# A three-layer kernel on one core: another order for its prologue, and two VectorE operations of the first blocks on GpSimd

## The chip, the cores and the metric

The kernel runs on one core of a Trainium2 chip. The metric is the device time of one execution in microseconds, as the median of several runs. A core has five engines with a queue each: TensorE (matrix products into PSUM), VectorE and ScalarE (element by element, on SBUF and PSUM), GpSimd (element by element, on SBUF), and SyncE, whose queue issues the transfers between HBM and SBUF. A queue issues in order. Engines wait for one another through semaphores, which the framework sets.

## The reference

Three layers in float32: chunked attention over 4 x 8 heads of 768 positions, then a layer with a squared ReLU, then a gated one.

```python
for c in range(nc):                       # chunks of 32; q, k, v: (4, 8, 768, 64)
    ...
    k_full = concatenate([mem_k, k_ctx], axis=2)      # 8 memory keys + up to 56 of the context
    scores = scale * matmul(q_c, k_full.T)
    a = exp(scores - max(scores))
    a = a / (sum(a) + 1e-9)
    out[:, :, c_start:c_end] = matmul(a, v_full)
x = out.transpose(0, 2, 1, 3).reshape(3072, 512)
h = maximum(x @ w_in, 0); y = (h * h) @ w_out         # 512 -> 2048 -> 512
g = y @ w_gate; z = (g * sigmoid(g) * (y @ w_val)) @ w_out2   # 512 -> 1536 -> 512
```

## The kernel before

Each large product is made of three products of float32r numbers: an operand is split into a high half (a cast, on ScalarE) and a low half (the difference, a subtraction), and high x high, high x low and low x high are summed in PSUM. In the names `whi`/`wlo` are the halves of a weight, `xh`/`xl` those of x, `gh`/`gl` those of the square. `split` (line 74) makes both halves: the cast is line 76, the subtraction line 79, whoever calls it.

**Attention.** The 32 groups of 96 queries are units; four units make a block of 384 tokens, and there are eight blocks. A unit u has these steps, each a function: `at_load` (queries and keys, 464 KB, one tile `qk`), `at_load_v` (values, 256 KB, two tiles), `at_scores` (48 small products, line 136; then VectorE's fills of masked columns), `at_max` (VectorE: maximum and its scaling, lines 148 and 149), `at_exp` (ScalarE: eight exponentials with their sums, line 157), `at_norm` (VectorE: two small instructions for the inverse sums, lines 171 and 172, and the multiplication of the probabilities by them, line 173), `at_turn` (VectorE: seven transposes of 32x32 blocks into `pT`, line 178), `at_pv` (16 products, line 197, into `abank`), `at_split_x` (ScalarE copies x out of `abank`, VectorE forms its low half). Probabilities have two tiles in turn; `abank` has one place for the weighted sum. Scores of the first block's units lie in two other PSUM tiles in turn, those of later units in `abank`.

**The first feed-forward layer.** For each block t and each of 16 slices f of 128 hidden columns, `hidden(t, f)` makes 12 products (line 264), then ScalarE applies ReLU (line 271), squares it twice (272, a float32r value, and 273), and VectorE subtracts for `gl` (line 274). `project(t, f)` makes 12 products (line 295), of which the last third uses `gl`. `hidden` runs two slices ahead of `project`. A slice's weight comes as 64-bit numbers: `load_w` fetches 1 MB into one of two tiles `raw` (line 84), `convert` turns it to float32 by an activation on ScalarE (line 94), a shift (line 95) and a combination (line 97) on VectorE, called a cut here, into one of two tiles `cut`; `split` then makes the 2 x 1024 columns of `whi` and `wlo`. `load1(f)` and `prep1(f)` do this for slice f; all 16 pairs of weights stay in SBUF through the eight blocks, in the 32 tiles of the pool `wp`. `spare()` takes a tile of this pool for something else.

**What sets the order.** Python code emits the instructions, and the framework's scheduler orders them by priority (the earlier emitted first) and by its own estimate of when an instruction is ready. Inside a region `manual_schedule` the engines that it names issue in the order of emission; where other instructions fall between these stays the scheduler's. Before, such a region held TensorE from block 1 on and all engines in the gated layer. The prologue (lines 541 to 562) emits, unit by unit, the four units of block 0, the loads of the first weights and `prep1(0)`. After it, before the first `hidden`, come the plans' steps below zero: `plan` holds the attention of the units 4 to 31, `wplan` the weights. Four steps make a round of one `hidden` and one `project`; a unit's steps stand at fixed lags (`LAGS`) about its step `e` (line 232): loading 24 before, scores 16 before, maximum 14 before, weighted sum at 0. For the units 4 to 7 (block 1), whose attention runs in block 0, e is 1, 17, 33 and 49. `prep1(f)` stands at step 4(f - 4), four rounds ahead of its use, for f of 1 to 3 at the start.

The gated layer (lines 427 and on) has GpSimd form the low halves of its weights (`split_w`, 128x512 and 128x384).

Of the kernel before, what the change touches and what calls it, by code (L numbers as in the profile page):

```python
# [7 lines left out]
F32 = mybir.dt.float32  # L8
# [3 lines left out]
ALU = mybir.AluOpType  # L12
# [6 lines left out]
GQ = 96  # L19
# [3 lines left out]
NH = 8  # L23
# [24 lines left out]
def attention_moe_moe_kernel(ctx, tc, att, w1, w2, out):  # L48
# [25 lines left out]
    def split(hi, lo, src, hi_engine, lo_engine):  # L74
        if hi_engine is act:
            act.copy(hi, src)  # L76
        else:
            hi_engine.tensor_copy(hi, src)
        lo_engine.tensor_tensor(lo, src, hi.bitcast(F32), ALU.subtract)  # L79
# [31 lines left out]

    def at_load(u):
        t, g = units[u]
        raw = st[u]["raw"] = ap.tile([128, UQ + UK], F32, tag="qk", name="qk")
        sp.dma_start(out=raw, in_=att[g, :, 0:UQ + UK])

    def at_load_v(u):
# [50 lines left out]
    def at_norm(u):  # L168
        sm = st[u].pop("sm")
        p = probs[u % 2][:, :, 0:WK]  # L170
        dve.tensor_scalar(sm, sm, 1e-9, None, ALU.add)
        dve.reciprocal(sm, sm)
        dve.tensor_tensor(p, p, sm.to_broadcast([GQ, NH, WK]), ALU.mult)  # L173

    def at_turn(u, chunks=range(3)):
        for c in chunks:
# [52 lines left out]
    nunit = BLOCKS[0]  # L229
    for t, n in enumerate(BLOCKS[1:], 1):  # L230
        for j in range(n):
            e = QB * (t - 1) + (j + 1) * QB // n - 15
            for lag, fn in LAGS:
                plan.setdefault(e + lag, []).append((lag, fn, nunit))
            nunit += 1
# [10 lines left out]
    def pair(pool_, tag):  # L246
        return [pool_.tile([128, 1024], R, tag=tag, name=n) for n in ("whi", "wlo")]

    def load1(f):
        w["raw", f] = load_w(w1[f])  # L250

    def prep1(f):
        w[f] = pair(wp, "w")
        split(*w[f], convert(w.pop(("raw", f))), act, dve)

    def hidden(t, f, between):
        n = nt_of[t]
        whi, wlo = w[f]
        xh, xl = xt[t]
        hps = hbank[next(turn) % 2][:, 0:n]  # L260
        i = 0
        for wt, x in ((whi, xh), (whi, xl), (wlo, xh)):
            for k in range(KD):
                pe.matmul(hps, wt[:, k * 128:(k + 1) * 128], x[:, k, 0:n], start=i == 0, stop=i == 3 * KD - 1)  # L264
                i += 1
                if i == 6:
                    between()
        r = gp.tile([128, NTM], F32, tag="r", name="r", bufs=2)[:, 0:n]
        gh = gp.tile([128, NTM], R, tag="gh", name="gh", bufs=3)[:, 0:n]
        gl = gp.tile([128, NTM], R, tag="gl", name="gl", bufs=3)[:, 0:n]  # L270
        act.activation(r, hps, AF.Relu)  # L271
        act.activation(gh, r, AF.Square)
        act.activation(r, r, AF.Square)  # L273
        dve.tensor_tensor(gl, r, gh.bitcast(F32), ALU.subtract)  # L274
        gtile[t, f] = gh, gl

    yps = {}
# [232 lines left out]
        wplan.setdefault(hs, []).append((fn, args))  # L510

    n0 = BLOCKS[0]
    for f in range(1, NF1):
        step = 4 * (f - 4) if f > 3 else f - QB
        at(step, prep1, f)
        if f + 2 < NF1:
            at(step, load1, f + 2)
# [20 lines left out]
            fn(*args)  # L538


    at_load(0)
    at_load_v(0)
    load1(0)
    at_scores(0)
    at_max(0)
    at_exp(0)
    for u in range(n0):
        if u + 1 < n0:
            at_load(u + 1)
            at_scores(u + 1)  # L550
            at_max(u + 1)
        at_norm(u)
        at_turn(u)
        if u + 1 < n0:
            at_exp(u + 1)
            at_load_v(u + 1)
        at_pv(u)
        if u == 0:
            load1(1)
            prep1(0)  # L560
        at_split_x(u)
    load1(2)
    for hs in range(min(min(plan), min(wplan)), 0):
        side(hs)
    for i in range(lookahead):
# [125 lines left out]
```

## Time and profile before

| | us |
|---|---|
| median of 3 runs | 1196.08 (1194.66 to 1196.27) |
| the profiled execution | 1195.23 |
| its span on the core | 1193.5 |
| TensorE busy | 1150.7 (96%) |
| VectorE busy | 692.2 (58%) |
| ScalarE busy | 605.2 (51%) |
| GpSimd busy | 355.4 (30%) |

The profile is of one execution. Times in it are microseconds from the start of the span unless marked ns. PE is TensorE, DVE VectorE, ACT ScalarE, POOL GpSimd, SP SyncE; a q behind a name is the engine's own sequencer. L12 is line 12 of the kernel. An instruction is named by its line, operation and tiles (out<-in, without buffer numbers). A long span is read by stretches, since its mean hides which engine is late where: here the prologue up to the first product of `hidden` (at 44.99), block 0 (up to some 119), and the rest. In the idle time ahead of an instruction the profile names what released it.

### The profile page before, as it was taken

Reading aid. Unit: us, or ns where it says so; the run is one execution under the profiler, and the core shown is the slowest. Engines: PE = TensorE matmul, PEld = TensorE weight load, DVE = VectorE, ACT = ScalarE, POOL = GpSimd, SP = SyncE. Lnnn points to the kernel's source line nnn. Section 1 sums busy time; section 2 is a strip of 40 time slices with the busy share of each in tenths; the row PEclk is TensorE's granted clock in tenths of the full one; section 3 lists DMA queues with packets and bytes.
Section 4 is the critical chain, followed back from the end, with each engine's and each line's share of the span. In section 5 each row is a group of like instructions: output and inputs, shape, how many; then the busy total and the mean of one; then the engine's idle time right before and its main releaser. Section 6 shows DMA issues by size and latency. Waiting matters only on the chain.

```text
span 1193.5 us, 20592 instructions
## 1 busy us (share of the span) xinstructions
PE 1150.7 (96%) x8000; PEld 1094.5 (92%) x8000; DVE 692.2 (58%) x1239; ACT 605.2 (51%) x1518; POOL 355.4 (30%) x297
## 2 busy tenths in 40 slices
PE   2599999999999999999999999999999999999998
PEld 2599999999999999999999999999999999999997
DVE  7997444745546455443424576656766576665454
ACT  5686455655555555554643354444545444453442
POOL 0000000201102021000043465656555565654541
PEclk9999999999999999999999999999999999999999
DMA  7563113536345253430223323353234433343231
GB/s 274 193 227 121 52 51 125 211 103 211 108 143 196 87 179 139 159 120 1 71 80 111 127 96 95 125 189 106 85 128 150 146 107 102 107 136 128 92 99 53
DMA packets 49442, 150.24 MB, mean 126 GB/s; under 512 B 4800, under 2 KB 14528, under 8 KB 44992
## 3 DMA queue, kind: packets, MB, share of 16 engines
q1 hardware_dynamic: 49344, 148.92, 36.7%
q8 instruction: 63, 1.03, 0.4%
q14 instruction: 35, 0.29, 0.1%
HBM read 122.16 MB, written 26.74 MB: 125 GB/s over the span
## 4 chain that ended last, share of the span: by engine, by line
PE 89%; DVE 6%; DMA 2%; ACT 1%; issue 1%; SPq 0%; ACTq 0%; DVEq 0%
PE hbank L409 30%; PE yb L295 20%; PE hbank L264 20%; PE yb L483 11%; PE abank L483 6%; PE abank L197 2%; DVE pT L178 2%; DMA wraw<-in_w_dram 2%; PE abank L136 1%; DVE cut L97 1%; ACT prob L157 1%; DVE wlo L79 0%; DVE prob L173 0%; DVE wraw L95 0%; DMA qk<-in_att_dram 0%
## 5 line engine op out<-in xcount | busy, mean ns | idle before, releaser
L79 POOL TENSOR_TENSOR wlo<-gvraw,whi 128x512 fp32r<-128x512 f32 x192 | 252.2, 1333 | 296.5 <-ACT whi L76 224.9
L264 PE MATMUL hbank<-x,whi 128*128 128x384 f32 x1024 | 200.2, 337 | 1.5 <-ACT r L271 0.9
L274 DVE TENSOR_TENSOR gl<-r,gh 128x384 fp32r<-128x384 f32 x128 | 77.4, 607 | 183.8 <-ACT r L273 183.4
L264 PEld LDWEIGHTS hbank<-x,whi 128*128 128x128 f32 x1024 | 180.5, 189 | 2.3 <-ACT r L271 1.2
L328 POOL TENSOR_TENSOR wraw<-cut 128x256 f32<-128x256 f32 x24 | 20.0, 852 | 461.6 <-DVE mx L149 260.8
L418 ACT CAST uh<-tmp 128x384 fp32r<-128x384 f32 x96 | 49.4, 515 | 211.4 <-DVE tmp L456 178.2
L271 ACT ACTIVATE r<-hbank 128x384 f32<-128x384 f32 x128 | 63.0, 492 | 152.2 <-PE hbank L264 151.0
L409 PE MATMUL hbank<-wlo,whi 128*128 128x384 f32 x480 | 124.9, 341 | 0.0
L409 PE MATMUL hbank<-whi,wlo 128*128 128x384 f32 x480 | 123.5, 338 | 0.0
L409 PE MATMUL hbank<-whi 128*128 128x384 f32 x480 | 122.5, 337 | 0.1
L295 PE MATMUL yb<-gh,whi 128*128 128x384 f32 x512 | 116.3, 341 | 0.0
L295 PE MATMUL yb<-gl,whi 128*128 128x384 f32 x512 | 113.4, 335 | 0.0
L295 PE MATMUL yb<-gh,wlo 128*128 128x384 f32 x512 | 113.4, 335 | 0.0
L264 PE MATMUL hbank<-x,wlo 128*128 128x384 f32 x512 | 109.7, 335 | 0.0
L409 PEld LDWEIGHTS hbank<-whi 128*128 128x128 f32 x480 | 90.0, 188 | 19.9 <-DVE tmp L451 0.4
L76 ACT CAST whi<-gvraw 128x512 fp32r<-128x512 f32 x192 | 99.2, 564 | 3.9 <-DMA gvraw<-w2g 2.5
L178 DVE STREAM_TRANSPOSE pT<-prob 32x256 f32<-32x256 f32 x224 | 97.3, 434 | 3.6
L295 PEld LDWEIGHTS yb<-gh,whi 128*128 128x128 f32 x512 | 89.3, 188 | 2.5
L295 PEld LDWEIGHTS yb<-gh,wlo 128*128 128x128 f32 x512 | 91.1, 188 | 0.0
L295 PEld LDWEIGHTS yb<-gl,whi 128*128 128x128 f32 x512 | 90.9, 188 | 0.1
L264 PEld LDWEIGHTS hbank<-x,wlo 128*128 128x128 f32 x512 | 90.7, 188 | 0.0
L157 ACT ACTIVATE prob<-abank,mx 96x72 f32<-96x72 f32 x224 | 68.3, 318 | 40.5 <-DVE mx L149 40.5
(90 smaller groups left out, 2061.8 us busy)
## 6 DMA issues: line engine op xcount, KB each, us to landing
wraw<-in_w_dram SPq DMA_DIRECT2D x34, 1024.0 KB, 6.2
gvraw<-w2g SPq DMA_DIRECT2D x48, 512.0 KB, 3.5
gvraw<-w2g SPq DMA_DIRECT2D x48, 384.0 KB, 3.1
qk<-in_att_dram SPq DMA_DIRECT2D x32, 464.0 KB, 4.5
spare<-w2o SPq DMA_DIRECT2D x24, 512.0 KB, 4.5
v<-in_att_dram SPq DMA_DIRECT2D x32, 256.0 KB, 3.4
y1d<-ys SPq DMA_DIRECT2D x8, 768.0 KB, 3.8
w2g<-wraw SPq DMA_DIRECT2D x12, 512.0 KB, 3.1
```

The costliest lines, as they stand in the source:

```text
L76: act.copy(hi, src)
L79: lo_engine.tensor_tensor(lo, src, hi.bitcast(F32), ALU.subtract)
L157: act.activation(probs[u % 2][:, h, 0:WK], s["s"][:, r, i], AF.Exp, bias=s["mx"][:, r, i:i + 1], scale=SCALE, accum_out=s["sm"][:, h],)
L178: dve.transpose(pT[row:row + 32, :, 32 * c:32 * c + 32], probs[u % 2][32 * c:32 * c + 32, :, col:col + 32],)
L197: pe.matmul(o[r:r + D, h // NI, h % NI // 2], s["v"][:, h * D:(h + 1) * D], pT[:, h], start=True, stop=True, tile_position=(0, r),)
L264: pe.matmul(hps, wt[:, k * 128:(k + 1) * 128], x[:, k, 0:n], start=i == 0, stop=i == 3 * KD - 1)
L271: act.activation(r, hps, AF.Relu)
L274: dve.tensor_tensor(gl, r, gh.bitcast(F32), ALU.subtract)
L295: pe.matmul(y[e], wt[:, c:c + 128], g, start=f == 0 and p == 0, stop=f == NF1 - 1 and p == 2)
L409: pe.matmul(to, wt[:, k * 128:k * 128 + 128], z[:, k], start=n == 0, stop=n == 5)
L418: act.copy(uh, u)
L483: pe.matmul(outs[j], u[:, c:c + 128], wt, start=f == 0 and p == 0, stop=f == NF2 - 1 and p == 2)
```

## The change

- The prologue stands in a region in which all five engines issue in the order of emission. Its steps are emitted in another order: four loads of queries and keys, two of values and two of weights first; scores and maxima of units 0 and 1; then for each unit the inverse sums, the split of the unit before, scores of the unit after next, transposes, weighted sum, and maximum and exponentials of the unit after next. The conversion of weight 0 (`cut1(0)`) stands behind unit 0's inverse sums, its split behind unit 1; weight 1 is cut and split at the end, weights 2 and 3 are loaded. Low halves of the weights 0 and 1 are GpSimd's.
- Keys and queries of block 0 go to spare tiles of the weight pool instead of the one tile `qk`.
- The multiplication by the inverse sums of blocks 0 and 1 (units 0 to 7) is GpSimd's.
- The low half of the square in block 0 is GpSimd's.
- The units 4 to 7 stand at e = 9, 23, 37 and 51.

```diff
--- before.py
+++ after.py
@@ -111,7 +111,8 @@
 
     def at_load(u):
         t, g = units[u]
-        raw = st[u]["raw"] = ap.tile([128, UQ + UK], F32, tag="qk", name="qk")
+        raw = spare()[:, 0:UQ + UK] if t == 0 else ap.tile([128, UQ + UK], F32, tag="qk", name="qk")
+        st[u]["raw"] = raw
         sp.dma_start(out=raw, in_=att[g, :, 0:UQ + UK])
 
     def at_load_v(u):
@@ -170,7 +171,9 @@
         p = probs[u % 2][:, :, 0:WK]
         dve.tensor_scalar(sm, sm, 1e-9, None, ALU.add)
         dve.reciprocal(sm, sm)
-        dve.tensor_tensor(p, p, sm.to_broadcast([GQ, NH, WK]), ALU.mult)
+
+        engine = pool if units[u][0] < 2 else dve
+        engine.tensor_tensor(p, p, sm.to_broadcast([GQ, NH, WK]), ALU.mult)
 
     def at_turn(u, chunks=range(3)):
         for c in chunks:
@@ -229,7 +232,7 @@
     nunit = BLOCKS[0]
     for t, n in enumerate(BLOCKS[1:], 1):
         for j in range(n):
-            e = QB * (t - 1) + (j + 1) * QB // n - 15
+            e = QB * (t - 1) + (j + 1) * QB // n - 15 if t > 1 else 14 * j + 9
             for lag, fn in LAGS:
                 plan.setdefault(e + lag, []).append((lag, fn, nunit))
             nunit += 1
@@ -249,9 +252,16 @@
     def load1(f):
         w["raw", f] = load_w(w1[f])
 
+    def cut1(f):
+        w["cut", f] = convert(w.pop(("raw", f)))
+
+    def split1(f, lo_engine):
+        w[f] = pair(wp, "w")
+        split(*w[f], w.pop(("cut", f)), act, lo_engine)
+
     def prep1(f):
-        w[f] = pair(wp, "w")
-        split(*w[f], convert(w.pop(("raw", f))), act, dve)
+        cut1(f)
+        split1(f, dve)
 
     def hidden(t, f, between):
         n = nt_of[t]
@@ -271,7 +281,7 @@
         act.activation(r, hps, AF.Relu)
         act.activation(gh, r, AF.Square)
         act.activation(r, r, AF.Square)
-        dve.tensor_tensor(gl, r, gh.bitcast(F32), ALU.subtract)
+        (pool if t == 0 else dve).tensor_tensor(gl, r, gh.bitcast(F32), ALU.subtract)
         gtile[t, f] = gh, gl
 
     yps = {}
@@ -510,7 +520,7 @@
         wplan.setdefault(hs, []).append((fn, args))
 
     n0 = BLOCKS[0]
-    for f in range(1, NF1):
+    for f in range(2, NF1):
         step = 4 * (f - 4) if f > 3 else f - QB
         at(step, prep1, f)
         if f + 2 < NF1:
@@ -538,28 +548,43 @@
             fn(*args)
 
 
+    early = ExitStack()
+    early.enter_context(tc.manual_schedule(engines={e.engine for e in (pe, act, dve, pool, sp)}))
     at_load(0)
     at_load_v(0)
+    at_load(1)
     load1(0)
-    at_scores(0)
-    at_max(0)
+    at_load_v(1)
+    at_load(2)
+    load1(1)
+    at_load(3)
+    for u in range(2):
+        at_scores(u)
+        at_max(u)
     at_exp(0)
     for u in range(n0):
-        if u + 1 < n0:
-            at_load(u + 1)
-            at_scores(u + 1)
-            at_max(u + 1)
         at_norm(u)
+        if u > 0:
+            at_split_x(u - 1)
+        if u == 0:
+            cut1(0)
+            at_exp(1)
+        if u + 2 < n0:
+            at_scores(u + 2)
         at_turn(u)
-        if u + 1 < n0:
-            at_exp(u + 1)
-            at_load_v(u + 1)
         at_pv(u)
-        if u == 0:
-            load1(1)
-            prep1(0)
-        at_split_x(u)
-    load1(2)
+        if u + 2 < n0:
+            at_load_v(u + 2)
+            at_max(u + 2)
+            at_exp(u + 2)
+        if u == 1:
+            split1(0, pool)
+            load1(2)
+    cut1(1)
+    at_split_x(n0 - 1)
+    split1(1, pool)
+    load1(3)
+    early.close()
     for hs in range(min(min(plan), min(wplan)), 0):
         side(hs)
     for i in range(lookahead):
```

## Rows read from the trace of the kernel before

**Rows 1.** Three stretches: busy PE, PEld, DVE, ACT, POOL; PEclk, DMA share, GB/s.

```profile
0.00:44.99 44.99, 10.50 (x256) 8.52 (x256) 37.59 (x72) 24.75 (x82) 1.37 (x8) 1.00 0.68 246
...
44.99:111.22 66.23, 64.35 (x565) 61.98 (x565) 59.71 (x99) 53.92 (x133) 0.00 (x0) 1.00 0.51 188
111.22:1193.50 1082.28, 1075.84 (x7180) 1024.03 (x7180) 594.87 (x1070) 526.56 (x1304) 354.06 (x289) 1.00 0.35 117
```

**Rows 2.** Waits of TensorE before 45 us: total, times, longest.

```profile
PE abank L197 <- DVE pT L178: 22.0, 4, 6.9
```

**Rows 3.** Groups of instructions before 45 us: busy, mean ns of one, idle before.

```profile
L178 DVE STREAM_TRANSPOSE pT<-prob 32x256 f32<-32x256 f32 x28 | 12.1, 434 | 0.4
L94 ACT ACTIVATE wraw<-wraw 128x1024 f32<-128x1024 f32 x7 | 8.0, 1154 | 3.2 <-DMA wraw<-in_w_dram 3.2
L97 DVE SCALAR_TENSOR_TENSOR cut<-wraw 128x1024 int32<-128x1024 int32 x6 | 7.3, 1211 | 0.1
L76 ACT CAST whi<-cut 128x1024 fp32r<-128x1024 f32 x5 | 5.2, 1049 | 3.7 <-DVE cut L97 3.7
L148 DVE TENSOR_REDUCE mx<-yb 96x8 f32<-96x576 f32 x4 | 3.0, 748 | 0.1
```

**Rows 4.** Chain (first row) and order of time in the prologue: start, us, what.

```profile
7.16 2.51 ACT prob L157 x16
...
4.68 1.09 PE L136 MATMUL yb<-qk 64*32 64x64 f32 x48 [4.68 <-DMA qk<-in_att_dram]
8.58 0.70 DVE L95 TENSOR_SCALAR wraw<-wraw 128x1024 int32<-128x1024 int32 x1 [1.52 <-DMA wraw<-in_w_dram]
9.90 0.20 DVE L172 RECIPROCAL sm<-sm 96x8 f32<-96x8 f32 x1
17.74 0.48 ACT L76 CAST x<-abank 128x384 fp32r<-128x384 f32 x1 [0.88 <-PE abank L197]
18.25 0.56 DVE L79 TENSOR_TENSOR x<-abank,x 128x384 fp32r<-128x384 f32 x1 [0.30 <-ACT x L76]
42.87 1.55 PE L197 MATMUL abank<-pT,v 128*64 128x96 f32 x16 [6.95 <-DVE pT L178]
44.99 2.29 PE L264 MATMUL hbank<-x,whi 128*128 128x384 f32 x6 [0.58 <-ACT x L76]
```

**Rows 5.** Subtractions on GpSimd in the gated layer: shortest, median, longest ns.

```profile
L79 POOL TENSOR_TENSOR wlo<-gvraw,whi x192: 997/1286/2018, 596.5 to 1167.2; 128x512 fp32r<-128x512 f32 x96, 128x384 fp32r<-128x384 f32 x96
L79 POOL TENSOR_TENSOR wlo<-spare,whi x48: 1282/1296/1689, 604.8 to 1157.8; 128x512 fp32r<-128x512 f32 x48
```

**Rows 6.** VectorE and GpSimd in the gated layer, in order of time.

```profile
647.21 1.29 POOL L79 TENSOR_TENSOR wlo<-spare,whi 128x512 fp32r<-128x512 f32 x1
647.99 0.92 DVE L456 TENSOR_TENSOR tmp<-tmp 128x384 f32<-128x384 f32 x1
...
814.85 1.69 POOL L79 TENSOR_TENSOR wlo<-gvraw,whi 128x512 fp32r<-128x512 f32 x1 [4.18 <-ACT whi L76]
```

**Rows 7.** TensorE in block 0: a wait (total, times, longest), two rows in time.

```profile
PE abank L197 <- DVE pT L178: 1.9, 2, 1.6
...
52.05 1.55 PE L264 MATMUL hbank<-x,whi 128*128 128x384 f32 x8
114.91 1.55 PE L264 MATMUL hbank<-x,whi 128*128 128x384 f32 x8
```

**Rows 8.** VectorE's groups from 44.99 to 111.22, and the last weight's low half.

```profile
L274 DVE TENSOR_TENSOR gl<-r,gh 128x384 fp32r<-128x384 f32 x14 | 7.6, 550 | 2.6 <-ACT r L273 2.5
L173 DVE TENSOR_TENSOR prob<-prob,sm 96x576 f32<-96x576 f32 x4 | 3.0, 754 | 0.1
...
106.45 1.22 DVE L79 TENSOR_TENSOR wlo<-cut,whi 128x1024 fp32r<-128x1024 f32 x1
```

**Rows 9.** DMA: a weight's load, us to landing; SP's waits up to 130 us.

```profile
wraw<-in_w_dram SPq DMA_DIRECT2D x34, 1024.0 KB, 6.2
...
SPq L84 <- DVE cut L97: 44.9, 13, 10.2
```

## The prediction, made before the changed kernel was built

> **What bounds the kernel now.** I read the stretches first: TensorE is busy 10.5 of the first 44.99 us, 64.35 of the next 66.2 and 1075.8 of the last 1082.3 [rows 1]. Of the 42.8 us in which it does nothing, 34.5 lie ahead of the first product of the hidden layer, 1.9 in block 0 and 6.4 in all the rest. The change touches only the first two stretches, and there alone time can be won. I then read who TensorE waits for: in the first stretch 22.0 us for the transposes of the probabilities, in four waits [rows 2]. So the prologue is a chain of units in which VectorE stands last. VectorE is busy 37.59 of those 44.99 us [rows 1], but only part of it is attention: six weights are already cut there and five cast [rows 3], of which the first product needs one. These were put between a unit's steps. In block 0 VectorE (59.7 of 66.2 us) and ScalarE (53.9) are nearly full while TensorE runs on [rows 1]; it waits 1.9 us for them, twice, for transposes [rows 7].
>
> **Prologue: the chain of the new order.** All five engines now issue these instructions in the order of the text. I follow each queue with the durations of before. Per unit: seven transposes of 0.434 [rows 3], 3.15 with the gaps; maximum and its scaling 0.9, of which the reduction is 0.75 [rows 3]; eight exponentials 2.5 [rows 4]; copy of x 0.5 and its low half 0.55; from the first instruction of the weighted sum to the product behind its copy 2.12 (42.87 to 44.99) [rows 4].
>
> GpSimd's prices are not in the prologue of before. Its subtractions took 0.997 us at 384 columns at the least, and 1.29 at 512 [rows 5]: 2.29 ns a column, so 1.44 for the 96x576 product by the inverse sums (0.75 on VectorE [rows 8] and 2.0, the longest of the group [rows 5], are the bounds) and 2.5 for a low half of 1024 columns (bounds 1.2, VectorE's own [rows 8], and 4.0, twice the longest). The operand that is repeated by a zero step appears on GpSimd nowhere; I take the slope.
>
> Start: unit 0's inverse sums are ready at 10.1 as before [rows 4]. The product goes to GpSimd, 10.2 to 11.65. Weight 0 landed at 8.58 behind 1744 KB, and now unit 1's 464 KB go ahead of it; at the pace of what landed between 4.68, when unit 0's scores start, and 8.58 [rows 4] (1280 KB, about 328 KB/us) that is 1.4 us, so 10.0. Its cut (0.70 and 1.21 on VectorE [rows 3, 4]) is now in front of unit 0's transposes, and both of these VectorE instructions collide with GpSimd (below): the cut ends at 13.45, or 12.4 if they don't. Then transposes to 16.6, maximum of unit 2 to 17.5, its exponentials to 19.95. Only now ScalarE gets to the copy of unit 0's x (20.5); its low half, 21.05, holds the transposes of unit 1 back: to 24.2. Maximum of unit 3 to 25.1, exponentials to 27.6, the cast of weight 0 (1.05 [rows 3]) to 28.65, its low half on GpSimd to 31.2, and **only behind it** unit 2's product, to 32.65: GpSimd's queue, not VectorE, is late here, by some 3 us. Transposes of unit 2 to 35.8, weighted sum, copy and low half to 38.45 (unit 3's product ends at 37.7, hidden), transposes of unit 3 to 41.6, and 2.12 plus a wait later the first product: 43.8. Against 44.99 that is **1.2 us earlier**. VectorE stands idle for some 11 us of it, waiting now for ScalarE and GpSimd.
>
> Bounds: 1.05 earlier without the collision at the start, and 2.0 earlier again if GpSimd were as fast as VectorE in the low half and the product on the chain; later by 2.1 for GpSimd at its longest in these two, by 0.85 if the queue serves unit 1's keys together with weight 0, by 1.1 if the scheduler puts the cut of weight 2 (0.70 and 1.21), which stands outside the ordered region, in front of transposes. So 40.7 to 47.8, all taken together. The four loads through spare weight tiles cost nothing where all is well: each tile is given back when its scores are done, long before weight 14 wants it; keys no longer wait for one tile. SP's queue waits for the two weighted sums (loads of v, two tiles) and behind them hold the loads of weights 2 and 3; weight 2 is issued near 26 and lands 6.2 later [rows 9], which costs nothing before the first product.
>
> **Block 0.** The first two products and unit 4's scores took 7.06 us (44.99 to 52.05 [rows 4, 7]); I leave that. What is new is the lead: two or three weights are cut at the first product, where it was six. From 52.05 to 114.91 TensorE ran 13 rounds [rows 7], 4.7 us each without the 1.9 of waits. Weight 3 is issued at the latest when weight 1 is cut (43.5): landing 49.7, ScalarE's step 1.15, cut 1.21, cast 1.05 [rows 3]: 53.1, where its product comes at 43.8 + 7.06 + 4.7 = 55.6. From there two tiles turn over in 6.2+1.15+1.2 = 8.6 us [rows 3, 9], 4.3 a weight against 4.7: the lead of 2.5 holds. SP's loads of weights waited 44.9 us for cuts before [rows 9], so this loop is real; a cut that is 0.8 us later in each round would eat the lead in three.
>
> VectorE gains and loses in this stretch: two more cuts, three more low halves and three more shifts, 2 x 1.21 + 3 x 1.22 + 3 x 0.70 [rows 3, 4, 8] = +8.2; the low halves of the square (7.6) and the products (3.0) go [rows 8]: -10.6. Net -2.4, and on GpSimd 16 x 1.0 + 4 x 1.44 + 2.5 = 24.3 us. Its cover is an engine that was idle (0.00 busy [rows 1]); the low half of the square is used by the last third of the projection two products later, over 4 us away.
>
> Against this stands the **collision**. Later in the kernel a VectorE multiply of two operands in SBUF began at 647.99, within a GpSimd subtraction that ran 647.21 to 648.50, and took 0.92 where 0.55 is usual for two operands of this size [rows 8]: +0.36; and a GpSimd subtraction that began with such a VectorE instruction took 1.69, not 1.29: +0.40 [rows 6]. Twenty-one GpSimd instructions in block 0, of which some 0.7 meet a cut, shift or low half (42 of VectorE's 57 us), at 0.36 each: 5.3 us. I take this, for it is from rows of the same kind; bounds 0 and 0.7 x 24.3 = 17.
>
> The Trainium skill ("SBUF — State Buffer", section "Who interferes with whom") calls the pair of ports that VectorE shares with GpSimd an exclusive lock: the later one fully blocks until the first is done, if the VectorE instruction has two SBUF inputs or runs in a two-port mode. The rows agree: the multiply ended 0.41 after the subtraction. By that rule the 17 us would be the sum, and the third case below holds.
>
> What VectorE can afford: the last low half of a weight ended at 107.7 [rows 8], its product started at 114.9. Start and waits 2.8 earlier, that product comes at 112.1 and uses the low half 1.4 later, 113.5; VectorE is done at 107.7 - 1.2 - 2.4 = 104.1 plus collisions. Up to 9.4 us of them are covered. Of the 1.9 us of waits for transposes I let 0.3 stand: the units now come 14 steps apart, unit 7 two steps later, the multiply is 0.7 longer but neither it nor the low halves queue on VectorE. Bounds 0 and 2.5.
>
> **Sum.** -1.2 (first product) -1.6 (waits in block 0) = -2.8. The profiled execution took 1195.23, with a span of 1193.5: 1192.4. It was 0.85 below the median 1196.08, against which the next median is held, so 1193.3. What a measurement of this kernel can tell from no change is about 0.2%, 2.4 us.
>
> **The rivals.** (1) *The order only moves the waits*: the chain above has idle VectorE in four places, each a new wait for ScalarE or GpSimd; with the later ends of two bounds the first product comes at 45 and block 0 keeps its 1.9 us. Time: 1196; from 1193.7 to 1198.4 in all. For it: the chain gains only 1.2 of 34.5, though 13 us of cuts left VectorE's prologue. Against: waits in block 0 came from a VectorE queue that gets shorter. (2) *GpSimd's lock makes VectorE the bound of block 0*: collisions cost 17 us, 7.6 beyond the cover, so -2.8+7.6 = +4.8, 1200.9; it is slower by over 0.2% from 14.6 us of collisions on. For it: the lead in weights is smaller by three, ScalarE has three more weights to convert (2.2 each) in 53.9 of 66.2. Against: 15 us of VectorE's work there, transposes above all, reads no second operand in SBUF, and the rows show 0.36 for a meeting. (3) *The region doesn't hold the order* (later weights are put in front of transposes as before): first product at 45, but no gl on VectorE: 1195; it lies within the first rival.
>
> **How the numbers follow.** Forecast, 0.45: 1193.3, its own range 1190.0 (the lowest bound, 40.7, and no waits: 4.3 + 1.9 = 6.2 less) to 1193.7. First rival with the third, 0.35. Second, 0.20. Faster 0.45, same 0.35, slower 0.20. The range, 1190 to 1200, leaves out the upper part of the second case.
>
> **What would show it.** First product near 43.8; unit 2's transposes released by GpSimd near 32.6; exponentials of unit 2 ahead of the first copy of x. In block 0: two-operand VectorE instructions longer than 1.22 and shifts longer than 0.70 where GpSimd is busy; TensorE waiting under 1 us for transposes. I am wrong if the first product is later than 45, if TensorE waits in block 0 for a cast or low half of a weight, or if a load of weights lands after its product is due.

## The result: 0.9% slower

| | before | changed |
|---|---|---|
| median, same chip | 1195.37 us | 1206.20 us |
| ratio of the two | | 1.0087 [1.0074, 1.0101] |
| repeated on another chip (`a_again`) | 1194.90 us | 1206.06 us, 1.0090 [1.0069, 1.0110] |

The forecast was 1193.3 in a range of 1190 to 1200: wrong in sign and in range. The profile of the changed kernel is taken from `a_again`, the same kernel run once more (1204.88 us, span 1203.0), because in the execution profiled first (2927.20 us, one of the four behind the median of 1206.20; the other three took 1204.66 to 1206.24) every product took about 2.6 times as long.

I cut the span as before: up to the first product of the hidden layer, then block 0 (here up to the first product of its last projection, slice 15, at 136.04; in the kernel before that is at 125.31), then the rest. The columns are busy PE, PEld, DVE, ACT and POOL, granted clock, DMA share, GB/s. First the changed kernel:

```profile
0.00:42.77 42.77, 10.51 (x257) 8.56 (x257) 24.93 (x57) 17.40 (x75) 8.64 (x13) 1.00 0.45 161
42.77:136.04 93.27, 82.24 (x700) 75.78 (x701) 76.38 (x104) 65.92 (x163) 27.15 (x21) 1.00 0.52 187
136.04:1203.00 1066.96, 1061.65 (x7045) 1010.07 (x7044) 590.40 (x1054) 521.05 (x1281) 352.88 (x289) 1.00 0.35 118
```

and block 0 and the rest of the kernel before, cut at the same products:

```profile
44.99:125.31 80.32, 78.44 (x700) 75.86 (x701) 67.37 (x116) 59.84 (x156) 0.00 (x0) 1.00 0.45 165
125.31:1193.50 1068.19, 1061.74 (x7045) 1010.15 (x7044) 587.20 (x1052) 520.64 (x1281) 354.06 (x289) 1.00 0.35 118
```

The prologue is 2.2 shorter, block 0 is 13.0 longer, the rest 1.2 shorter: +9.5, the difference of the spans. The loss is all in block 0. Both kernels run the same 700 instructions of TensorE there. Its idle time grew from 1.9 to 11.0 (+9.2), and it was busy 3.8 longer with the same products. Who TensorE waited for, from the first product to the start of block 1 (total, times, longest; the counterpart of [rows 7]):

```profile
PE hbank L274 <- DVE wlo L79: 3.5, 3, 1.6
PE abank L200 <- DVE abank L145: 1.9, 1, 1.9
PE hbank L274 <- ACT r L281: 1.5, 2, 1.0
PE hbank L274 <- ACT whi L76: 1.2, 1, 1.2
PE abank L200 <- DVE pT L181: 1.1, 1, 1.1
PE abank L200 <- DVE abank L143: 0.9, 1, 0.9
PE yb L305 <- POOL gl L284: 0.8, 1, 0.8
PE hbank L274 <- ACT x L76: 0.6, 1, 0.6
```

(In the changed kernel a line stands 1 to 10 lower than before: the hidden layer's product is L274, the projection L305, `gl` L284, transposes L181, the weighted sum L200.) Before, the stage had waits for transposes and one copy of x. Now 4.7 us are for halves of a weight (L79 on VectorE, the cast L76), which before was never waited for here. 2.8 are for fills of masked columns (L143, L145): with the new steps the scores of unit u+1 and the fill behind them are emitted ahead of the weighted sum of u. Both write `abank`, so the weighted sum has to wait for a fill that is late in VectorE's queue.

The prologue's chain in order of time (the counterpart of [rows 4]):

```profile
28.23 2.34 POOL L79 TENSOR_TENSOR wlo<-cut,whi 128x1024 fp32r<-128x1024 f32 x1 [9.63 <-ACT whi L76]
30.53 1.14 POOL L176 TENSOR_TENSOR prob<-prob,sm 96x576 f32<-96x576 f32 x1
31.70 3.13 DVE L181 STREAM_TRANSPOSE pT<-prob 32x256 f32<-32x256 f32 x7 [2.59 <-POOL prob L176]
42.77 1.65 PE L274 MATMUL hbank<-x,whi 128*128 128x384 f32 x4 [0.58 <-ACT x L76]
```

Unit 2's product stands behind the low half of weight 0 in GpSimd's queue, VectorE waits 2.59 for it, and the transposes follow: as forecast, 1 us earlier throughout.

Instructions from 43 to 125 us (busy, mean ns, idle before), beside [rows 3, 8]:

```profile
L79 DVE TENSOR_TENSOR wlo<-cut,whi 128x1024 fp32r<-128x1024 f32 x14 | 21.5, 1542 | 1.4 <-ACT whi L76 1.3
L97 DVE SCALAR_TENSOR_TENSOR cut<-wraw 128x1024 int32<-128x1024 int32 x14 | 20.4, 1456 | 2.2 <-ACT wraw L94 1.7
L284 POOL TENSOR_TENSOR gl<-r,gh 128x384 fp32r<-128x384 f32 x15 | 18.5, 1233 | 39.5 <-ACT r L283 21.0 <-issue 18.5
L95 DVE TENSOR_SCALAR wraw<-wraw 128x1024 int32<-128x1024 int32 x13 | 9.9, 763 | 3.0 <-DMA wraw<-in_w_dram 2.9
L150 DVE TENSOR_SCALAR mx<-mx 96x8 f32<-96x8 f32 x4 | 1.9, 478 | 0.0
```

In the kernel before, without a collision, these are 1.22, 1.22, 0.69 and 0.16. The excess is 14 x 0.32 + 14 x 0.24 + 13 x 0.07 + 4 x 0.32 = 10.0 us. How a late weight and a collision meet is seen in order of time, for weights 14 and 15:

```profile
113.75 1.75 DVE L97 SCALAR_TENSOR_TENSOR cut<-wraw 128x1024 int32<-128x1024 int32 x1 [0.62 <-ACT wraw L94]
115.42 1.77 DVE L181 STREAM_TRANSPOSE pT<-prob 32x256 f32<-32x256 f32 x4
115.53 1.04 ACT L76 CAST whi<-cut 128x1024 fp32r<-128x1024 f32 x1
116.63 1.68 PE L274 MATMUL hbank<-x,whi 128*128 128x384 f32 x8 [1.16 <-ACT whi L76]
117.14 1.01 POOL L284 TENSOR_TENSOR gl<-r,gh 128x384 fp32r<-128x384 f32 x1 [2.72 <-ACT r L283]
117.23 1.47 DVE L95 TENSOR_SCALAR wraw<-wraw 128x1024 int32<-128x1024 int32 x1
118.62 1.21 DVE L79 TENSOR_TENSOR wlo<-cut,whi 128x1024 fp32r<-128x1024 f32 x1
118.63 2.07 POOL L284 TENSOR_TENSOR gl<-r,gh 128x384 fp32r<-128x384 f32 x1 [0.48 <-ACT r L283]
119.76 2.03 DVE L97 SCALAR_TENSOR_TENSOR cut<-wraw 128x1024 int32<-128x1024 int32 x1
119.89 0.97 PE L274 MATMUL hbank<-x,wlo 128*128 128x384 f32 x4 [1.58 <-DVE wlo L79]
```

Weight 14 is cut at 113.75 to 115.5 beside GpSimd's product (113.27, 1.15), and the cast follows at once: TensorE waits 1.16 for it. The low half then stands behind four transposes and a shift that GpSimd's subtraction drew out to 1.47: TensorE waits 1.58. That low half, on VectorE from 118.62, holds GpSimd's next subtraction up (2.07 instead of 1.0), and this in turn the cut of weight 15 (2.03 instead of 1.22). The kernel before had its last low half done at 107.7, 7 us before the products of its slice began [rows 7, 8].

### The profile page after: what moved, and what is told of

Same layout as the page of the kernel before. It is cut to its first block, busy times and chain, and to the rows that moved or that the text cites. A ratio compares the mean times of both kernels' runs of the same rounds, so it can differ in the third digit from the quotient of the medians.

```text
span 2925.4 us, 20606 instructions
## 1 busy us (share of the span) xinstructions
PE 2890.4 (99%) x8000; PEld 2149.1 (73%) x8000; DVE 668.9 (23%) x1213; ACT 612.7 (21%) x1518; POOL 343.2 (12%) x323
## 4 chain that ended last, share of the span: by engine, by line
PE 99%; DVE 0%; issue 0%; DMA 0%; POOL 0%; ACT 0%; SPq 0%; DVEq 0%; POOLq 0%
PE hbank L419 31%; PE yb L305 24%; PE hbank L274 23%; PE yb L493 12%; PE abank L493 6%; PE abank L200 2%; PE abank L137 1%; DVE pT L181 0%; DMA wraw<-in_w_dram 0%; POOL wlo L79 0%; POOL prob L176 0%; DVE cut L97 0%; ACT wraw L94 0%; ACT x L76 0%; SPq L116 0%
## 5 line engine op out<-in xcount | busy, mean ns | idle before, releaser
L274 PE MATMUL hbank<-x,whi 128*128 128x384 f32 x1024 | 488.0, 677 | 0.6 <-ACT x L76 0.6
L274 PEld LDWEIGHTS hbank<-x,whi 128*128 128x128 f32 x1024 | 354.2, 348 | 94.7 <-issue 82.6
L79 POOL TENSOR_TENSOR wlo<-gvraw,whi 128x512 fp32r<-128x512 f32 x192 | 214.4, 1138 | 1142.1 <-ACT whi L76 596.6
L419 PE MATMUL hbank<-whi 128*128 128x384 f32 x480 | 270.1, 679 | 0.0
L305 PE MATMUL yb<-gh,wlo 128*128 128x384 f32 x512 | 264.5, 670 | 0.0
L305 PE MATMUL yb<-gl,whi 128*128 128x384 f32 x512 | 264.5, 684 | 0.0
L305 PE MATMUL yb<-gh,whi 128*128 128x384 f32 x512 | 263.7, 687 | 0.0
L274 PE MATMUL hbank<-x,wlo 128*128 128x384 f32 x512 | 258.7, 689 | 0.0
L284 DVE TENSOR_TENSOR gl<-r,gh 128x384 fp32r<-128x384 f32 x112 | 62.4, 557 | 854.1 <-ACT r L283 854.1
L274 PEld LDWEIGHTS hbank<-x,wlo 128*128 128x128 f32 x512 | 187.6, 369 | 48.0 <-issue 42.8
L305 PEld LDWEIGHTS yb<-gl,whi 128*128 128x128 f32 x512 | 178.4, 350 | 59.0 <-issue 55.2
L305 PEld LDWEIGHTS yb<-gh,wlo 128*128 128x128 f32 x512 | 173.3, 340 | 50.8 <-issue 40.7
L305 PEld LDWEIGHTS yb<-gh,whi 128*128 128x128 f32 x512 | 178.1, 359 | 43.5 <-issue 39.6
L419 PEld LDWEIGHTS hbank<-whi,wlo 128*128 128x128 f32 x480 | 168.3, 352 | 47.0 <-issue 42.2
L419 PEld LDWEIGHTS hbank<-wlo,whi 128*128 128x128 f32 x480 | 167.8, 351 | 47.3 <-issue 41.9
L419 PE MATMUL hbank<-z,whi 128*128 128x384 f32 x384 | 193.8, 679 | 0.0
```

The source lines that it names most:

```text
L284: (pool if t == 0 else dve).tensor_tensor(gl, r, gh.bitcast(F32), ALU.subtract)
L305: pe.matmul(y[e], wt[:, c:c + 128], g, start=f == 0 and p == 0, stop=f == NF1 - 1 and p == 2)
L419: pe.matmul(to, wt[:, k * 128:k * 128 + 128], z[:, k], start=n == 0, stop=n == 5)
```

## The experiments

The question was which part costs what: the *order* (fewer weights cut at the first product), the *collisions* of GpSimd with VectorE, the *steps* of the units 4 to 7; and, once the weights were seen to be late, whether they are late for their *transfer* or for VectorE's *queue*. "First product" and "block 0" are read in the order of time of each profiled execution as above; the rest of the kernel was 1066.8 to 1069.1 in all twelve, so at most 2.3 us of a difference can lie there. A profiled execution need not be a typical one: it lies above its median by 3.0 us in `a_steps`, 4.1 in `a_lead_new`, 2.0 in `b_idle` and 1.7 in `a_dve_steps`. And in `b_pool`, `b_idle` and `a_lead_new` TensorE ran some microseconds of block 0 at the lower of its two clock levels (last section): the same 700 products kept it busy 2.1 and 1.6 us longer than in the kernel before, and 3.0 longer than in `a_lead`.

| kernel | median | its before | ratio | first product | block 0 |
|---|---|---|---|---|---|
| before | | | 1 | 44.99 | 80.3 |
| a_again | 1206.06 | 1194.90 | 1.0090 [1.0069, 1.0110] | 42.77 | 93.3 |
| a_dve | 1196.74 | 1194.90 | 1.0013 [1.0003, 1.0022] | 39.89 | 87.6 |
| a_steps | 1200.41 | 1194.90 | 1.0045 [1.0033, 1.0056] | 42.88 | 90.7 |
| b_pool | 1200.79 | 1194.90 | 1.0041 [1.0028, 1.0055] | 46.76 | 84.2 |
| a_gl | 1200.53 | 1194.77 | 1.0053 [1.0039, 1.0068] | 42.86 | 88.3 |
| a_dve_steps | 1197.03 | 1194.77 | 1.0016 [1.0003, 1.0029] | 39.84 | 88.8 |
| b_idle | 1197.09 | 1194.77 | 1.0026 [1.0014, 1.0038] | 45.04 | 84.3 |
| a_lead | 1192.10 | 1194.77 | 0.9985 [0.9969, 1.0001] | 39.87 | 84.2 |
| a_lead_gl | 1194.77 | 1195.06 | 0.9993 [0.9983, 1.0003] | 39.62 | 85.0 |
| a_lead_new | 1192.76 | 1195.06 | 0.9976 [0.9966, 0.9986] | 39.63 | 88.0 |
| a_noturn | 1189.94 | 1195.06 | 0.9953 [0.9937, 0.9969] | 40.08 | 79.9 |

**The changed kernel again** (`a_again`), no edit.

> The changed kernel once more, for an undisturbed trace (in the one at hand every TensorE product took 2.6 times its usual time, so only its prologue can be read: first product at 43.6). Theory Lock (collisions of GpSimd with VectorE make VectorE late in block 0): first product near 43.6 to 44, TensorE's idle time in block 0 (from the first product to the first product of block 1) 10 us or more above the 1.9 of before, all the rest as before. Theory Clock (TensorE is granted its low clock over a stretch): idle time as before, but a stretch in which 12 products take twice the 2.08 us, and a mean granted clock below 1 there. Theory Later (the scheduler places something else differently in blocks 1 to 7): block 0 as before, the difference spread over the blocks behind. Ratio to before 1.008 to 1.010 in all three.

It repeated the loss, all of it in block 0, with the clock at 1.00 there; its trace is the one read above. TensorE's idle time grew by 9.2, a little less than the 10 that Theory Lock asked for.

**Both operations back on VectorE** (`a_dve`): order and steps stay.

```diff
-        engine = pool if units[u][0] < 2 else dve
+        engine = dve
...
-        (pool if t == 0 else dve).tensor_tensor(gl, r, gh.bitcast(F32), ALU.subtract)
+        dve.tensor_tensor(gl, r, gh.bitcast(F32), ALU.subtract)
```

> The changed kernel with the products by the inverse sums and the low halves of the square back on VectorE; the order of the prologue, the low halves of the first two weights on GpSimd, the spare tiles and the new steps of the units 4 to 7 stay. Lock: GpSimd does nothing behind the prologue, so the collisions are gone; VectorE has 10.6 us more of its own work. Faster than the changed kernel by 4 us or more. Clock and Later: within 2 us of the changed kernel, apart from the first product, which moves by under 2 us.

The first product came at 39.89, 2.9 earlier than with GpSimd in the chain, 5.1 earlier than before; block 0 was 5.7 shorter than in the changed kernel. Of the loss of 11.2 us GpSimd's part is 9.3, where Theory Lock had asked for 4 or more. But block 0 is still 7.3 longer than before, with hardly a collision left in it (GpSimd works there for 2.9 us, on weight 1; VectorE's low halves take 1243 ns, 1217 before): the order, with the new steps, costs there more than it wins in front.

**Old steps** (`a_steps`): units 4 to 7 again at 1, 17, 33 and 49.

```diff
-            e = QB * (t - 1) + (j + 1) * QB // n - 15 if t > 1 else 14 * j + 9
+            e = QB * (t - 1) + (j + 1) * QB // n - 15
```

> The changed kernel with the units 4 to 7 at their old steps (1, 17, 33, 49). If the new steps are to blame (unit 4 to 7 too late or scores ahead of the sum in the one tile), it is near 1196; Lock: within 2 us of the changed kernel, 1204 to 1208; Clock: the same.

5.7 us came back, of the medians of one chip, so the total fell between the two theories. The waits for fills (2.8) are gone and half of the excess with them (low half 1433, cut 1342 ns). In its profiled execution, which is 3.0 above its median, block 0 is only 2.6 shorter; where the rest of the 5.7 went I can't show.

**The reverse: GpSimd's two operations in the kernel before** (`b_pool`).

```diff
-        dve.tensor_tensor(p, p, sm.to_broadcast([GQ, NH, WK]), ALU.mult)
+        (pool if units[u][0] < 2 else dve).tensor_tensor(p, p, sm.to_broadcast([GQ, NH, WK]), ALU.mult)
...
-        dve.tensor_tensor(gl, r, gh.bitcast(F32), ALU.subtract)
+        (pool if t == 0 else dve).tensor_tensor(gl, r, gh.bitcast(F32), ALU.subtract)
```

> The kernel before with the two GpSimd parts alone: products by the inverse sums of the units 0 to 7 and the low halves of the square of block 0. Lock: 1200 to 1206, the loss of block 0 without the new order of the prologue. Clock, if it comes from the new prologue: within 2 us of 1196. Forecast of my sum for this part alone: -1.6 in block 0, and the prologue later by 4 x 0.7.

+5.9, of which 1.8 in front of the first product and 3.9 in block 0. Half of the 3.9 (2.1) is TensorE's longer busy time at the lower clock. TensorE now waits there once for GpSimd's subtraction itself:

```profile
PE yb L295 <- POOL gl L274: 1.8, 1, 1.8
```

So "two products later" was no full cover for it. The offload loses in the old order too, where my sum had forecast 1.6 less in block 0.

**GpSimd only for the product** (`a_gl`): `gl` back on VectorE, the product by the inverse sums stays.

```diff
-        (pool if t == 0 else dve).tensor_tensor(gl, r, gh.bitcast(F32), ALU.subtract)
+        dve.tensor_tensor(gl, r, gh.bitcast(F32), ALU.subtract)
```

> The changed kernel with the low halves of the square back on VectorE; the products by the inverse sums stay on GpSimd. With both back it was 9.3 us faster. Lock: most of it comes from the 15 subtractions in block 0; first product near 42.8, total 1198 to 1201. Chain: the products by the inverse sums cost the most (three of them on the prologue's chain): total near 1204.

With `a_dve` and `a_again` this parts the loss, each against its own before and all with the new steps: order +1.8, the product +3.9 (3.0 of it ahead of the first product), the low halves of the square +5.4 (all in block 0). The total lies in the range of Theory Lock. The shift is back at 685 ns, the cut at 1341.

**Both on VectorE and old steps** (`a_dve_steps`): the edits of `a_dve` and `a_steps` together.

> Both parts of GpSimd's back on VectorE and the old steps of the units 4 to 7: what is left is the order of the prologue, two low halves on GpSimd and the spare tiles. First product near 39.9, 5.1 us ahead of before. Theory Lead (weights are cut at 5.5 us each against 4.7 for a round, so a lead of two or three at the first product does not last the block, where six did): block 0 still gives 3 us or more of the 5.1 back, TensorE waiting for casts and low halves of weights; total 1192 to 1195. Theory Steps (the new steps alone gave it back): total near 1190 to 1191.

No different from `a_dve`: the steps cost nothing measurable by themselves, only together with GpSimd's two operations. The total lies above the ranges of both theories: block 0 gave back 8.5 us, more than the 5.1 won in front. TensorE waited there 3.5 us for casts and low halves, as Theory Lead has it, and 1.9 for transposes. What remains is the order alone, +2.3.

Read across the table, GpSimd's two operations cost 5.9 us in the old order with its lead of six weights (`b_pool`), some 3 in the new order with the old steps (`a_steps` less `a_dve_steps`, each against its before) and 9.3 with the new steps (`a_again` less `a_dve`). So a long lead did not make them cheaper; the new steps made them dearer.

Here the weights are seen almost without collisions. In order of time, from ScalarE's step on weight 4:

```profile
50.92 1.16 ACT L94 ACTIVATE wraw<-wraw 128x1024 f32<-128x1024 f32 x1
...
51.58 3.12 DVE L181 STREAM_TRANSPOSE pT<-prob 32x256 f32<-32x256 f32 x7
...
54.73 1.03 DVE L284 TENSOR_TENSOR gl<-r,gh 128x384 fp32r<-128x384 f32 x2
...
55.67 1.29 DVE L95 TENSOR_SCALAR wraw<-wraw 128x1024 int32<-128x1024 int32 x2
...
56.88 1.22 DVE L97 SCALAR_TENSOR_TENSOR cut<-wraw 128x1024 int32<-128x1024 int32 x1
```

Weight 4 has landed and ScalarE's step on it ends at 52.1; its cut begins at 56.9, behind a unit's seven transposes, two subtractions and two shifts. The tile `raw` is given back only after that, and the load of weight 6 is issued at 58.16. From the cut of weight 3 (47.89) to that of 15 (115.78) it took 67.9 us: 5.66 a weight.

**Unused work on GpSimd** (`b_idle`): the kernel before with 16 subtractions on GpSimd in block 0 that nobody waits for.

```diff
         gtile[t, f] = gh, gl
+        if t == 0:
+            pool.tensor_tensor(waste[:, 0:n], gh.bitcast(F32), gh.bitcast(F32), ALU.subtract)
...
+    waste = ap.tile([128, NTM], F32, name="waste")
```

> The kernel before, with 16 more subtractions of 128x384 on GpSimd in block 0, one for each slice, that read the float32r square and write a tile that nothing reads. No result of the kernel waits for them. Lock: VectorE's cuts, low halves and shifts in block 0 become longer by 3 us or more in sum, and the kernel slower by 1 to 5 us. Theory Chain (GpSimd only hands its results over later): the same time as before, within 1 us, and the same durations on VectorE.

+2.3 us, for work that nobody waits for. Groups of GpSimd and VectorE from 43 to 125, and all of TensorE's waits from 46 to 129:

```profile
L277 POOL TENSOR_TENSOR waste<-gh 128x384 f32<-128x384 f32 x16 | 15.7, 980 | 106.8 <-ACT gh L272 106.7
L97 DVE SCALAR_TENSOR_TENSOR cut<-wraw 128x1024 int32<-128x1024 int32 x11 | 14.5, 1319 | 0.7 <-ACT wraw L94 0.2
L274 DVE TENSOR_TENSOR gl<-r,gh 128x384 fp32r<-128x384 f32 x16 | 9.3, 593 | 2.3 <-ACT r L273 2.2
```
```profile
PE abank L197 <- DVE pT L178: 4.2, 3, 2.5
```

Cuts are 0.10 longer than the 1.22 of before, `gl` 0.04 than the 0.55 [rows 8], shifts 0.05 (742 instead of 688 ns), low halves are as before: 2.3 us in sum, under the 3 that Theory Lock asked for in cuts, low halves and shifts. So collisions alone make a kernel slower that has its lead in weights. TensorE waits there for no weight. The delay seems to reach it through the transposes, which stand in the same queue and have no lead: 4.2 us instead of 1.9 [rows 7]. In the profiled execution the longest of these waits was followed by the lower clock, a further 1.6.

**The lead given back** (`a_lead`): `a_dve_steps`, but weights 1 to 3 are cut within the prologue, each ScalarE step and each cut at a place where its engine stood idle; the loads of 2 to 5 are issued there, and GpSimd forms three low halves.

```diff
         if u > 0:
+            if u < 3:
+                cut_dve(u)
             at_split_x(u - 1)
         if u == 0:
             cut1(0)
+            load1(2)
             at_exp(1)
...
+        if u == 1:
+            load1(3)
+            split1(1, pool)
+        if u == 2:
+            load1(4)
+            split1(2, pool)
         at_turn(u)
         at_pv(u)
+        if u == 0:
+            split1(0, pool)
         if u + 2 < n0:
             at_load_v(u + 2)
+            cut_act(u + 1)
...
-        if u == 1:
-            split1(0, pool)
-            load1(2)
-    cut1(1)
+        if u == 2:
+            cut_act(3)
+    cut_dve(3)
     at_split_x(n0 - 1)
-    split1(1, pool)
-    load1(3)
+    load1(5)
```

(`cut_act` is ScalarE's step of `convert`, `cut_dve` the two of VectorE; the split of weight 3 stands at step -1.)

> As the one with old steps and both parts on VectorE, with the weights 1, 2 and 3 cut within the prologue: ScalarE's step and VectorE's two instructions of each stand where these engines waited, loads of the weights 2 to 5 are issued as soon as a tile is cut, the cast of weight 0 goes ahead of unit 2's exponentials, three low halves on GpSimd. Lead: four weights cut at the first product, which comes at 38 to 40; block 0 loses under 2 us; total 1189 to 1191. If VectorE's queue, not the lead, is the limit of block 0, the gain over the one with old steps is under 1.5 us.

The first product stayed at 39.87, so the added cuts cost nothing in front, and block 0 fell from 88.8 to 84.2. Against `a_dve_steps` on the same chip that is -4.9 us in the medians. Giving the lead back took away about half of the order's loss in block 0 (4.6 of 8.5). The rest stayed: block 0 still loses 3.9 where I expected under 2, the total is above 1191, and TensorE still waits 2.5 us for casts and low halves, late in the block.

**The lead, with `gl` on GpSimd** (`a_lead_gl`): `a_lead`, with line `gl` as in the changed kernel.

> The version with weights cut ahead (1192.1), with block 0's low halves of the square on GpSimd again. My prediction held that a lead of weights covers up to 9 us of collisions. If it does, this is within 1 us of 1192.1, for the lead is back. If block 0 has no slack in VectorE's queue even so, it is slower by 3 to 5.5 us, as the same step was from a_gl to the changed kernel (5.5).

The ratio went from 0.9985 to 0.9993 with overlapping intervals (+1.0 us), the median against its before from -2.7 to -0.3 (+2.4; the two ran on different chips). That lies between the two expectations. The same line cost 5.4 in the changed kernel, but this does not show that the lead covers collisions, for there were fewer of them: low halves took 1290 ns, cuts 1298, shifts 785, the scaling of the maxima 326, which is 3.5 us more in sum than in `a_lead`, where the changed kernel had 7.2 more than `a_gl`. Steps and products differ between the two pairs as well.

**The lead, with the new steps** (`a_lead_new`): `a_lead` with the steps 9, 23, 37 and 51.

> The version with weights cut ahead, with the new steps of the units 4 to 7 (9, 23, 37, 51) in place of the old ones. The steps did nothing measurable where no GpSimd work stood in block 0 (1196.7 against 1197.0): so within 1 us of 1192.1. If the later steps leave VectorE free for weights early in the block, up to 2 us faster.

-2.3 us, and the only complete version whose interval lies below 1. It doesn't part from `a_lead`, as expected. The 88.0 of its block 0 is of an execution 4.1 us above the median, in which TensorE waited 4.11 us at once for a fill and ran on at the lower clock (last section).

**Transposes left out** (`a_noturn`): `a_dve_steps` without the transposes of the units 4 to 7, so block 1 works on old probabilities.

```diff
     def at_turn(u, chunks=range(3)):
+        if units[u][0] == 1:
+            return
```

> The new order with both parts on VectorE and old steps (1197.0), leaving out the transposes of the units 4 to 7 (so block 1 works on old probabilities): 28 x 0.434 = 12.2 us less for VectorE in block 0, transfers and tiles as they are. Theory Queue (a weight's cut waits behind a unit's transposes in VectorE's queue, and the turn of its tile with it): two weights are cut in under 10 us instead of 11.3, and block 0 shrinks from 88.8 us by 4 or more; total 1191 to 1193. Theory Transfer (the 6.2 us from issue to landing and two tiles set the pace): cuts stay at 11 us for two, TensorE still waits 3 us for casts, total 1195 to 1197.

This takes 12.2 us off VectorE in block 0 and touches no load of a weight. Who TensorE waited for from 39 to 130:

```profile
PE hbank L276 <- ACT x L76: 0.6, 1, 0.6
PE hbank L276 <- ACT whi L76: 0.4, 1, 0.4
```

The cuts now came 4.49 us apart (48.69 to 102.57, weights 3 to 15) and block 0 took 79.9. With the transfers as they were the weights were on time: two of them in 9.0 us instead of 11.3, so the turn of the two tiles was long because the cut stood in VectorE's queue. That is Theory Queue; the total came 1.1 below its range. Whether the transposes hurt by their place or by their sum this run doesn't tell, since they are gone. In `a_dve_steps` VectorE is busy 75.95 of 88.80, so it was not full.

A third tile of `raw` or `cut`, which would lengthen the turn that can be borne, was not tried.

## Why the prediction was wrong, point by point

**Prologue: right.** "The first product: 43.8" was 42.77, and from the cut of weight 0 on each step came 0.5 to 1.1 us before its forecast. GpSimd's prices from a slope over the columns held: 1.14 to 1.54 for the product against 1.44, 2.34 for the low half on the chain against 2.5. GpSimd's queue, late "by some 3 us", cost 2.9 (`a_dve`). The chain's gain of 1.2 was 2.2: the collision at the start cost 0.2 instead of 1.05, and GpSimd's two instructions on the chain were 0.5 shorter.

**"The lead of 2.5 holds": the step that failed.** I added a load, ScalarE's step and a cut, 8.6 us for two tiles, "4.3 a weight against 4.7" [rows 3, 9], as if an instruction on VectorE began when its input was there. The load took less than I put (median 5.0 from issue to landing instead of 6.2), and yet the turn was 11.4: in the changed kernel the cuts of weights 3 to 15 were 5.7 us apart, on average (51.64 to 119.76). 11.4 less 5.0, 1.15 and 1.2 leaves 4 us in each turn standing in a queue. `a_noturn` shows which queue: without the transposes two cuts took 9.0 us. By this step the order, from which I had expected no wait for a weight, lost 7.3 us in block 0 (`a_dve`), and 3.9 with the lead given back (`a_lead`). The number to doubt it by was in the trace of before, where the cut of weight 5 begins at 44.78 and that of 15 at 102.20:

```profile
44.78 1.23 DVE L97 SCALAR_TENSOR_TENSOR cut<-wraw 128x1024 int32<-128x1024 int32 x1
...
102.20 1.23 DVE L97 SCALAR_TENSOR_TENSOR cut<-wraw 128x1024 int32<-128x1024 int32 x1
```

5.7 us a weight there too, a microsecond more than TensorE's round of 4.7. The kernel before lived on its lead of six weights: a cut ended 20.5 us ahead of its slice's first product at weight 5, and 11.5 ahead at weight 15. The change spent half of that lead in advance; there a cut was 2.0 us ahead at weight 3 and 1.1 at weight 5. What I had read in the prologue as six weights cut where one is needed was that lead.

**"Of the 1.9 us of waits for transposes I let 0.3 stand": wrong, in part by the same step.** All waits of block 0 together became 10.9 (without the copy of x ahead of the first product), 4.7 of it for halves of weights and 2.8 for fills that the new steps put in front of a weighted sum; the transposes kept 1.1. That TensorE "waits in block 0 for a cast or low half of a weight" I had named as what would prove me wrong. The steps, at which I had put no price, cost 5.7 us beside GpSimd's work (`a_steps`). The other 3.8 us of block 0, in which TensorE counts as busy, seem to come in the main with the pauses: four products of L274 after a wait took 0.97 where four without one take 0.85 (the row of 119.89 above is one), since their records overlap when they follow one another. I have not assigned these 3.8 one by one.

**"At 0.36 each: 5.3 us": mis-sized.** The collisions were 10.0. I counted a meeting for 0.7 of GpSimd's instructions and one victim each. In fact an instruction of GpSimd can meet two of VectorE's, one that it delays and one that delays it, as the subtraction of 118.63 did. And it delays the scaling of the maximum, which I had left out. **"Up to 9.4 us of them are covered": wrong**, because the cover was worked out for one result alone, the last low half, and with the lead of the kernel before. With a short lead cuts and low halves reach TensorE late (4.7 us). And with the long lead other results of VectorE's queue do, which have no lead: transposes in `b_idle`, and in `b_pool` `gl` itself. GpSimd's part of block 0's loss of 13.0 was 5.7 (`a_dve`), where I had put it at nothing.

**The rivals.** The second, the lock (once called "the third case"), had the sign and nothing else. Its condition was collisions beyond 14.6 us, and they were 10.0; its +4.8 (1200.9) was for 17 us of them, and the loss was +10.8. Fewer collisions cost more, since there was no such cover and the order lost as well. The first came near the order alone (1196 against 1197.03 in `a_dve_steps`), but by luck: the order won 5.1 us in front, where that rival saw nothing, and lost 8.5 behind. None of the three had what the runs show: a lead that does not last, collisions without the cover that I had given them, and new steps that make them dearer.

## What to carry to other kernels

Work that looks too early may be a lead: before taking it out, compare the pace of its refill in the same trace (first and last cut, divided by their number) with the pace at which it is used. For a loop over two tiles take this measured pace, not the sum of its instructions, since each step also stands in the queue of a busy engine. Moving two-operand work to an idle GpSimd is only free if what VectorE runs beside it can bear the delay; try it with the work unused first. A cover worked out for one result says nothing of the others that stand in the same queue.

## What the runs showed of the hardware

- Subtractions and cuts on VectorE and subtractions on GpSimd excluded each other for a whole instruction, both ways: GpSimd's subtraction of 118.63 ended 0.9 after VectorE's low half, the cut of 119.76 ended 1.1 after that. It reaches instructions with one input too. The scaling of 96x8 maxima (0.16 alone) that began at 70.17 during a GpSimd subtraction ended with it:

```profile
69.74 1.02 POOL L284 TENSOR_TENSOR gl<-r,gh 128x384 fp32r<-128x384 f32 x1 [4.83 <-issue]
```
```profile
70.17 0.62 DVE L150 TENSOR_SCALAR mx<-mx 96x8 f32<-96x8 f32 x1
```

  The Trainium skill ("SBUF — State Buffer", section "Who interferes with whom") names `tensor_scalar` among the operations that can take the shared pair of ports in a two-port mode; shifts of 763 instead of 690 ns and the 0.62 us above agree. Maxima and transposes (748 and 434 ns in both kernels) were not touched, though 11 transposes and two maxima ran beside a GpSimd instruction up to 140 us; nor was the low half of x, which reads one operand from PSUM (three beside GpSimd, 0.54 to 0.56 us).
- In `b_idle` a wait of 2.47 us for transposes ended with some 3.4 us at the lower of TensorE's two levels (0.50 granted, 1.2 GHz), up to 117.3: four products took 1.39 instead of 0.85 us. The columns are those of the stretches above:

```profile
112.00:114.00 2.00, 0.19 (x2) 0.19 (x4) 1.93 (x5) 1.06 (x3) 0.87 (x2) 0.96 0.01 4
114.00:116.00 2.00, 2.00 (x58) 1.78 (x62) 0.81 (x2) 0.00 (x0) 0.00 (x0) 0.50 0.03 8
116.00:118.00 2.00, 2.00 (x31) 1.83 (x19) 0.94 (x3) 0.48 (x1) 0.00 (x0) 0.69 0.69 153
```

  The clock fell in the same way at the end of a wait of 1.82 in `b_pool` (112 to 115.5) and within one of 4.11 in `a_lead_new` (96 to 103), but not at one of 1.91 in the changed kernel (before 103.99). In `a_lead_new`:

```profile
97.12 1.55 PE L200 MATMUL abank<-pT,v 128*64 128x96 f32 x16 [4.11 <-DVE abank L145]
...
100.04 1.48 PE L317 MATMUL yb<-gh,wlo 128*128 128x384 f32 x4
```

- The first products of the hidden layer run at about half rate in every kernel (four in 1.65 us at 42.77, against 0.85 later; in the kernel before six in 2.29 [rows 4]) although the granted clock of that stretch reads 1.00. Four of them took 1.48 at 46.81 in the changed kernel, as long as the four of `a_lead_new` above at 0.50. So they ran at the pace of the lower level; whether they ran at that level, which the record does not show, none of the runs tells.
